# Attention scores from float32r parts: Q and K split into high and rest from batch 1 on

## The chip, the cores and the metric

The kernel runs on one core of a Trainium2 chip. Its engines are TensorE (PE in the profile, with its weight loads as PEld), VectorE (DVE), ScalarE (ACT), GpSimd (POOL) and SyncE (SP, which only issues DMAs here). Each engine works through its own instructions in order, and semaphores tie them together. The metric is the device time of one execution in microseconds (us); before the change it is 1247.83 us, the median of 3 runs (1247.72 to 1249.23).

## The reference

Sparse attention, then a gated feed-forward block. For 8 batches of 8 heads, 576 tokens and head size 64:

```python
scores = (1.0 / np.sqrt(D)) * np.matmul(q, k.transpose(0, 1, 3, 2))
kth = np.partition(scores, -32, axis=-1)[..., -32:-31]
scores = np.where(scores >= kth, scores, -1000000000.0)   # the 32 largest of each row stay
attn = np.exp(scores - np.max(scores, axis=-1, keepdims=True))
attn = attn / (np.sum(attn, axis=-1, keepdims=True) + 1e-09)
x = np.matmul(attn, v)                  # heads side by side: 4608 x 512
a, b = x @ w1, x @ w2                   # 4608 x 1024 each
out = (a * b @ w3) @ w_out              # 4608 x 512
```

The scores decide which 32 keys of a row are kept, so they are needed at nearly the precision of float32.

## The kernel before, in words

**Slots and turns.** A head pair (two heads, in the lower and upper 64 partitions) is handled in tiles of 128 tokens. A batch's 576 tokens are cut in two parts, of 320 and of 256. A part of 320 gives each head pair two tiles of 128 and half of one that it shares with the next head pair (`t == 4`, where two pairs bring 64 tokens each); a part of 256 gives two tiles. So a batch has 18 slots, two of them with `t == 4`, and there are 144 slots in all. The main loop (L541) runs one turn per slot, with a pipeline over the turns: in turn p the scores of slot p+1 are computed, the 32 largest of slot p are searched, slot p-1 is masked and exponentiated, and slot p-2 is transposed and multiplied with V.

**What a turn does.** In the order of the code: GpSimd makes the two `edge` values of slot p-1 from its largest scores. ScalarE's two `pab<-s` activations and GpSimd's two `pab<-s,pab` subtractions are the masks (`mask`, L303), one for each head. TensorE transposes slot p-2 (`tp`, `ro<-ident`), and ScalarE copies the result (`pts`, `pr`). ScalarE's two `pab<-pab,edge` activations are the exponentials. Then come the scores of slot p+1 (`st`, two PSUM tiles, for keys 0 to 383 and 384 to 575), their copies by ScalarE to `s`, the products with V (`ro`), and GpSimd's `sums` and its two `pab<-pab,sums` (normalise). VectorE's search (`w`, `top`) is laid between these steps.

**What fills TensorE.** The feed-forward block of a finished part is a queue of matmuls (`ab` and `eo`). `fill` (L497) is called three times in a turn and issues products up to a share that is counted in columns (`SHARE`, L41), not in time. So the number and order of TensorE's instructions in a turn are fixed when the program is built. What is left in the queue after the last slot runs at the end.

**The precision of the products.** The feed-forward block already works on parts: a float32 value is split into a high part rounded to float32r (a cast by ScalarE) and the rest (a subtraction), and a product is the sum of three float32r products, high by high, high by rest and rest by high. The scores are plain float32 products (L227 and L230): the Q tile is the stationary operand, 64 partitions by 128 tokens, and the K tile is streamed, 384 or 192 columns. Each of them shows up as two MATMUL instructions in the trace, a float32r product as one.

**Loads and buffers.** `load_qk` (L198) fetches a unit (a head pair of a part) into `qt` and `kt` (three buffers each). Its call is two turns ahead of the turn that computes the unit's first scores, and SyncE, which only waits for free buffers and for outputs to store, runs ahead of that. The `z` pool (L84, four buffers of 128 x 1024) holds the encoded weights in the first part of the run, up to the last weight load.

Nearly all instructions are recorded through one helper, so that they stand under line 54 in the profile; tiles tell them apart.

Of the kernel before, what the change touches and what calls it, by code (L numbers as in the profile page):

```python
# [9 lines left out]
F32 = mybir.dt.float32  # L10
F32R = mybir.dt.float32r
# [3 lines left out]
ALU = mybir.AluOpType  # L15
# [3 lines left out]
B, H, S, D = 8, 8, 576, 64  # L19
# [4 lines left out]
NA, NB = 320, 256  # L24
PARTS = ((0, NA, (0, 1, 4)), (NA, NB, (2, 3)))
PLACE = {0: 0, 1: 128, 4: 256, 2: 0, 3: 128}
HEADS = slice(0, 64), slice(64, 128)
# [35 lines left out]
def attn_moe(ctx: ExitStack, tc: tile.TileContext, q, k, v, w1, w2, w3, w_out, out, flag, general):  # L63
# [12 lines left out]
    pe, act, dve, pool, sp = nc.tensor, nc.scalar, nc.vector, nc.gpsimd, nc.sync  # L76
# [7 lines left out]
    z_p = ctx.enter_context(tc.tile_pool(name="z", bufs=4))  # L84
# [21 lines left out]
    if not general:  # L106
        pe, act, dve, pool, sp = (InOrder(tc, e) for e in (pe, act, dve, pool, sp))
# [87 lines left out]
    def at(x, b, *i):  # L195
        return x[(b, *i)] if isinstance(b, int) else x[(ds(b, 1), *i)].rearrange("o p n -> (o p) n")

    def load_qk(b, part, hp):  # L198

        lo, n, _ = PARTS[part]  # L200
        qt = kq_p.tile([128, NA], F32, tag="q", name="qt")
        sp.dma_start(qt[:, :n], at(q, b, hp)[:, lo : lo + n])
        kt = kq_p.tile([128, S + 64], F32, tag="k", name="kt")
        sp.dma_start(kt, at(k, b, hp))
        return qt, kt

    def load_v(b, hp):

        vt = kq_p.tile([128, 11 * D], F32, tag="v", name="vt")
        sp.dma_start(vt, at(v, b, hp))  # L210
        return vt

    def scores(pairs, t):

        out = []
        for lo, hi in KEYS:  # L220
            st = ps_a.tile([128, 2, 512], F32, tag="a", name="st")
            for a in range(2):
                cut = slice(lo + 64, hi + 64) if a == 0 else slice(lo, hi)
                if t == 4:
                    qt, kt = pairs[a]
                    for i, p in enumerate(HEADS):
                        pe.matmul(st[HEADS[i ^ a], a, : hi - lo], qt[p, PLACE[4] : NA], kt[p, cut], start=True, stop=True)  # L227
                else:
                    (qt, kt), p, o = pairs[0], HEADS[a], PLACE[t]
                    pe.matmul(st[:, a, : hi - lo], qt[p, o : o + 128], kt[p, cut], start=True, stop=True)  # L230
            out.append(st)
        return out

    def new_s():
        return att_p.tile([128, 2, S], F32, tag="s", name="s", bufs=2)
# [11 lines left out]
    def top32_steps(s, st, taken, slot):  # L247

        w = att_p.tile([128, 2, S], F32, tag="w", name="w", bufs=1)
        top = tops[slot % len(tops)]
        one, two, three = slice(0, NG), slice(NG, 2 * NG), slice(2 * NG, S)
        in_two, in_three = st[0][:, :, NG : 2 * NG], st[1][:, :, :NG]
        dve.tensor_tensor(w[:, :, three], s[:, :, one], in_two, op=ALU.max)
        dve.tensor_tensor(w[:, :, two], s[:, :, one], in_two, op=ALU.min)
        yield  # L260
        ins = dve.tensor_tensor(w[:, :, one], w[:, :, three], in_three, op=ALU.max)
        behind(ins, taken, "one engine at a time reads a bank of the scores")
        dve.tensor_tensor(w[:, :, three], w[:, :, three], in_three, op=ALU.min)
        yield
        for i in range(4):
            cut = slice(i * 8, (i + 1) * 8)
            for a in range(2):
                dve.max(top[:, a, cut], w[:, a, one] if i < 3 else w[:, a, :])
                if i == 3 and a == 0:
                    yield  # L270
            if i < 3:
                for a in range(2):
                    dve.match_replace(w[:, a, one], top[:, a, cut], w[:, a, one], NEG)
                yield

    def edges_of(slot):
        top = tops[slot % len(tops)]
        edge = small.tile([128, 2, 2], F32, tag="edge", name="edge")
        pool.tensor_tensor(edge, top[:, :, 0:32:31], coef, op=ALU.mult)
        return edge  # L280

    def compare(slot):
        top = tops[slot % len(tops)]
        pool.tensor_tensor(over[:, 2 * slot : 2 * slot + 2], top[:, :, 31], top[:, :, 23], op=ALU.subtract)
# [15 lines left out]
    def new_weights():  # L300
        return att_p.tile([128, 2, S], F32, tag="pab", name="pab"), small.tile([128, 2], F32, tag="sums", name="sums")
# [54 lines left out]
    def places(xs, t):  # L356
        o = PLACE[t]
        if t == 4:
            return [(x, slice(o, o + 64), slice(j * 64, j * 64 + 64)) for j, x in enumerate(xs)]
        return [(xs[0], slice(o, o + 128), slice(0, 128))]  # L360
# [5 lines left out]
    def take_low(to, ov):  # L366
        for x, cols, n in to:
            dve.tensor_tensor(x[:, 1, cols], ov[:, n], x[:, 0, cols].bitcast(F32), op=ALU.subtract)
# [78 lines left out]
    if general:  # L447
# [3 lines left out]
        with tc.For_i(0, B, 1) as b:  # L451
            seen = small.tile([1, 1], I32, tag="seen", name="seen", bufs=1)
            nc.sync.dma_start(seen, flag[ds(b + 1, 1), :])
            with tc.If(nc.values_load(seen, min_val=0, max_val=1) > 0):
                for part in range(2):
                    qk, vts, xs = {}, {}, {}
                    for of, hps, t in SLOTS:
# [5 lines left out]
                        s, st = new_s(), scores([qk[hp] for hp in hps], t)  # L463
# [12 lines left out]
                        to = places([xs[hp] for hp in hps], t)  # L476
# [7 lines left out]
    units = list(dict.fromkeys(u for us, _ in slots for u in us))  # L484
    first = {u: next(i for i, (us, _) in enumerate(slots) if u in us) for u in units}
    final = {(b, part): max(i for i, (us, _) in enumerate(slots) if us[0][:2] == (b, part)) for b in range(B) for part in range(2)}
    qk, vts, ss, sts, edges, pabs, xts, lows = {}, {}, {}, {}, {}, {}, {}, {}
    queue = []

    put_off = []  # L490
    spare = 0

    def evict():
        while put_off:
            put_off.pop(0)()

    def fill(n):  # L497
        nonlocal spare
        evict()
        spare = spare + n if queue else 0  # L500
        while queue and spare > 0:
            cost = next(queue[0], None)
            if cost is None:
                queue.pop(0)
            elif not cost:
                spare = 0
            else:
                spare -= cost
# [32 lines left out]
    for p in range(-1, n_slots + 3):  # L541
        i, j, m = p + 1, p - 1, p - 2
        if i < n_slots:
            for u in units:
                if first[u] - 2 == i:
                    qk[u] = load_qk(*u)
                if first[u] == i:
                    vts[u] = load_v(u[0], u[2])
        finder = top32_steps(ss[p], *sts.pop(p), p) if 0 <= p < n_slots else iter(())
        if 0 <= j < n_slots:  # L550
            edges[j] = edges_of(j)
        next(finder, None)
        if m - 1 in lows:
            take_low(*lows.pop(m - 1))
            b, part, _ = slots[m - 1][0][0]
            if final[b, part] == m - 1:
                queue.append(moe_steps(b, part, [xts.pop((b, part, hp)) for hp in range(NHP)], put_off.append))
        next(finder, None)
        if p >= 0:
            warm()  # L560
        if 0 <= j < n_slots:
            pabs[j] = new_weights()
            for a in range(2):
                mask(ss[j], edges[j], pabs[j][0], a)
            compare(j)
        fill(SHARE[0])
        next(finder, None)
        if 0 <= m < n_slots:
            tp, ro = turn(pabs[m][0])
            pts, pr = take_turned(tp, ro)  # L570
        warm(False)
        if 0 <= j < n_slots:
            exps(edges[j], *pabs[j], 0)
            exps(edges[j], *pabs[j], 1)
            enlarge(pabs[j][1])
        weigh(2)
        fill(SHARE[1])
        next(finder, None)
        warm(False)
        if i < n_slots:  # L580
            st = scores([qk[u] for u in slots[i][0]], slots[i][1])
            ss[i] = new_s()
            take_scores(ss[i], st, 0)
            sts[i] = st, take_scores(ss[i], st, 1)
        if 0 <= m < n_slots:
            us, t = slots[m]
            for u in us:
                if u not in xts:
                    xts[u] = new_x()
            ov = values([vts[u] for u in us], t, pts, pr, ro)  # L590
            lows[m] = places([xts[u] for u in us], t), ov
            take_high(*lows[m])
        next(finder, None)
        warm()
        next(finder, None)
        if 0 <= j < n_slots:
            invert(pabs[j][1])
            normalise(*pabs[j])
        weigh(8)
        fill(SHARE[2])  # L600
        for _ in finder:
            pass
        if 0 <= m < n_slots:
            del ss[m], pabs[m], edges[m]
        warm()
# [62 lines left out]
```

## Time and profile before

| | us |
|---|---|
| median of 3 runs | 1247.83 |
| the profiled execution | 1246.48 |
| its span, first to last instruction | 1244.6 |
| TensorE busy in the span | 1202.3 (97%) |
| VectorE busy | 1137.1 (91%) |
| ScalarE busy | 941.0 (76%) |
| GpSimd busy | 869.4 (70%) |

The profiled execution lies 1.35 us under the median, and its span 1.88 us under its own time. The first two hundred microseconds or so hold batch 0 and the loading of the weights; after that the turns repeat, batch by batch. Busy time of TensorE is a loose measure, since matmuls are pipelined and their ends are modelled, so durations of products overlap; the distance from the start of one to the start of the next tells their pace.

### The profile page before, as it was taken

To read this page: it belongs to the slowest core of one execution; us is meant where nothing else is said; L and a number is where in the kernel's file an instruction comes from. 1 tells how busy PE (TensorE), PEld (TensorE's weight loads), DVE (VectorE), ACT (ScalarE), POOL (GpSimd) and SP (SyncE) were. 2 spreads that over 40 slices of the span, in tenths; PEclk is the share of its full clock that TensorE was granted. 3 is DMA by queue.
4 is the path that set the end of the run, shared out by engine and by line. 5 is a ranking of instruction groups with operands and counts; after the bars stand their busy time and mean duration, and the time that the engine had idled before them with its cause. 6 is when DMAs were issued, how large, how long until landed. Compare 5 with 4: busy or idle time off the path is not lost.

```text
span 1244.6 us, 29906 instructions
## 1 busy us (share of the span) xinstructions
PE 1202.3 (97%) x10513; PEld 1042.5 (84%) x10513; DVE 1137.1 (91%) x3963; ACT 941.0 (76%) x2025; POOL 869.4 (70%) x1218
## 2 busy tenths in 40 slices
PE   4889799999999999999999999999999999999998
PEld 2444678898888888898889988888888988888998
DVE  7999999999999999999999999999999999999910
ACT  6888877787877777777777777777877777777731
POOL 6899887776767677676767667676767677676721
PEclk9999899999999999999999999999999999999999
DMA  6545411202121211213121121202112111202000
GB/s 230 190 145 178 140 56 39 72 28 93 40 67 53 71 56 35 71 33 94 41 66 54 48 80 33 73 28 89 49 46 75 40 61 39 92 28 71 13 23 21
DMA packets 42802, 85.91 MB, mean 69 GB/s; under 512 B 4754, under 2 KB 21138, under 8 KB 42642
## 3 DMA queue, kind: packets, MB, share of 16 engines
q1 hardware_dynamic: 42642, 83.91, 21.1%
q8 instruction: 85, 1.39, 0.5%
q14 instruction: 75, 0.61, 0.2%
HBM read 74.45 MB, written 9.44 MB: 67 GB/s over the span
## 4 chain that ended last, share of the span: by engine, by line
PE 91%; DVE 3%; POOL 2%; ACT 2%; issue 1%; DMA 1%; SPq 0%; ACTq 0%; DVEq 0%
PE ab L54 33%; PE eo L54 17%; PE ro L54 15%; PE st L54 13%; PE tp L54 10%; PE pf L54 3%; POOL pab L54 1%; DVE w L54 1%; DVE top L54 1%; DVE y L54 1%; DVE wl L54 1%; POOL y L54 1%; ACT pab L54 0%; POOL wo L54 0%; ACT s L54 0%
## 5 line engine op out<-in xcount | busy, mean ns | idle before, releaser
L54 POOL TENSOR_TENSOR pab<-s,pab 128x576 f32<-128x576 f32 x288 | 406.3, 1432 | 118.9 <-ACT pab L54 118.9
L54 DVE MAX8 top<-w 128x8 f32<-128x192 f32 (+1 forms) x1152 | 477.9, 447 | 0.0
L54 PE MATMUL ab<-xf,wh 128*128 128x256 f32 (+1 forms) x2048 | 439.0, 302 | 3.3 <-ACT asb L54 3.0
L54 PEld LDWEIGHTS ab<-xf,wh 128*128 128x128 f32 x2048 | 333.7, 189 | 14.5 <-issue 8.9
L54 PE MATMUL ab<-xf,wl 128*128 128x256 f32 (+1 forms) x1024 | 308.0, 301 | 0.0
L54 ACT ACTIVATE pab<-s,edge 128x576 f32<-128x576 f32 x288 | 208.0, 770 | 123.1 <-POOL edge L54 123.1
L54 DVE MATCH_REPLACE8 w<-top,w 128x192 f32<-128x192 f32 x864 | 289.3, 342 | 0.0
L54 POOL TENSOR_SCALAR pab<-pab,sums 128x576 f32<-128x576 f32 x288 | 211.6, 748 | 32.8 <-DVE sums L54 32.8
L54 PE MATMUL eo<-g,wf 128*128 128x256 f32 (+1 forms) x1536 | 231.6, 301 | 0.0
L54 ACT COPY pts<-tp 128x1024 f32<-128x1024 f32 x144 | 146.1, 1014 | 106.4 <-PE tp L54 106.1
L54 ACT ACTIVATE pab<-pab,edge 128x576 f32<-128x576 f32 x288 | 222.0, 779 | 4.0 <-POOL pab L54 3.8
L54 PEld LDWEIGHTS eo<-g,wf 128*128 128x128 f32 x1536 | 208.4, 188 | 8.1 <-issue 7.5
L54 PEld LDWEIGHTS ab<-xf,wl 128*128 128x128 f32 x1024 | 193.8, 189 | 4.1 <-issue 4.1
L54 PE MATMUL st<-kt,qt 64*128 64x192 f32 (+3 forms) x1280 | 181.7, 433 | 6.9 <-DMA kt<-in_k 4.3
L54 ACT COPY s<-st 128x768 f32<-128x768 f32 (+1 forms) x288 | 170.5, 650 | 4.0 <-PE st L54 4.0
L54 PE MATMUL tp<-ident,pab 128*128 128x128 f32 x1152 | 151.5, 275 | 18.2 <-DVE w L54 18.2
L54 DVE TENSOR_TENSOR w<-s,st 128x384 f32<-128x384 f32 x288 | 146.5, 550 | 21.4 <-ACT s L54 6.9
L54 PEld LDWEIGHTS st<-kt,qt 64*128 64x128 f32 (+1 forms) x1280 | 97.6, 178 | 77.7 <-issue 17.0
L54 DVE TENSOR_TENSOR w<-w,st 128x384 f32<-128x384 f32 x288 | 157.9, 548 | 4.9
L54 PE MATMUL ro<-pts,vt 128*64 128x128 f32 (+1 forms) x2560 | 160.4, 268 | 0.0
L54 PEld LDWEIGHTS tp<-ident,pab 128*128 128x128 f32 x1152 | 133.8, 142 | 24.7 <-POOL pab L54 15.4
L54 PEld LDWEIGHTS ro<-pts,vt 128*64 128x64 f32 x2560 | 126.8, 137 | 33.1 <-issue 31.6
(48 smaller groups left out, 1097.8 us busy)
## 6 DMA issues: line engine op xcount, KB each, us to landing
vt<-in_v SPq DMA_DIRECT2D x64, 352.0 KB, 3.2
kt<-in_k SPq DMA_DIRECT2D x64, 320.0 KB, 3.9
z<-in_w SPq DMA_DIRECT2D x32, 512.0 KB, 3.7
qt<-in_q SPq DMA_DIRECT2D x32, 160.0 KB, 3.2
out_t<-osb SPq DMA_DIRECT2D x32, 160.0 KB, 1.8
z<-in_wo SPq DMA_DIRECT2D x8, 512.0 KB, 5.6
qt<-in_q SPq DMA_DIRECT2D x32, 128.0 KB, 3.2
out_t<-osb SPq DMA_DIRECT2D x32, 128.0 KB, 1.7
```

Source lines behind the costliest of these rows:

```text
L54: ins = fn(*args, **kw)
```

## The change

Batch 0 stays as it is. From batch 1 on each unit gets two more tiles, `hi` and `lo`, in the `z` pool (128 x 1024, float32r; K stands in columns 0 to 639, Q behind it). One turn before the turn that computes the unit's first scores, ScalarE casts K to `hi` ahead of the masks (`split_k`) and Q after them (`split_q`), and GpSimd writes K's rest to `lo` ahead of its masks (`rest_k`). In the turn of the scores itself GpSimd writes Q's rest, again ahead of its masks (`rest_q`). The scores of those units become three products for each head and each of the two key ranges; slots with `t == 4` keep the float32 products.

```diff
-        return qt, kt
+        return [qt, kt, None, None]
+    def split_k(n, unit):
+        unit[2:] = (z_p.tile([128, 1024], F32R, tag="z", name=name) for name in ("hi", "lo"))
+        act.copy(unit[2][:, : S + 64], unit[1])
+    def split_q(n, unit):
+        act.copy(unit[2][:, S + 64 : S + 64 + n], unit[0][:, :n])
+    def rest_k(n, unit):
+        pool.tensor_tensor(unit[3][:, : S + 64], unit[1], unit[2][:, : S + 64].bitcast(F32), op=ALU.subtract)
+    def rest_q(n, unit):
+        cut = slice(S + 64, S + 64 + n)
+        pool.tensor_tensor(unit[3][:, cut], unit[0][:, :n], unit[2][:, cut].bitcast(F32), op=ALU.subtract)
...
-                    (qt, kt), p, o = pairs[0], HEADS[a], PLACE[t]
-                    pe.matmul(st[:, a, : hi - lo], qt[p, o : o + 128], kt[p, cut], start=True, stop=True)
+                    jobs.append((st[:, a, : hi - lo], pairs[0], HEADS[a], slice(PLACE[t], PLACE[t] + 128), cut))
+            for k in range(3):
+                for to, (qt, kt, high, low), p, tokens, keys in jobs:
+                    if high is not None and t != 4:
+                        q_at = slice(S + 64 + tokens.start, S + 64 + tokens.stop)
+                        q_part, k_part = (low if k == 1 else high)[p, q_at], (low if k == 2 else high)[p, keys]
+                        pe.matmul(to, q_part, k_part, start=(k == 0), stop=(k == 2))
+                    elif k == 0:
+                        pe.matmul(to, qt[p, tokens], kt[p, keys], start=True, stop=True)
...
+    parted = [u for u in units if u[0] > 0]
...
+        for u in parted:
+            if first[u] - 1 == i:
+                split_k(PARTS[u[1]][1], qk[u])
+        for u in parted:
+            if first[u] - 1 == i:
+                rest_k(PARTS[u[1]][1], qk[u])
+        for u in parted:
+            if first[u] - 0 == i:
+                rest_q(PARTS[u[1]][1], qk[u])
...
+        for u in parted:
+            if first[u] - 1 == i:
+                split_q(PARTS[u[1]][1], qk[u])
```

The first fence is TensorE's order at the scores of the first slot of batch 1, before (-) and after (+). `x2` counts the two heads; a float32 row of the score is two instructions in the trace. `hi,lo` is K's high part by Q's rest, `lo,hi` K's rest by Q's high part.

```order
 L54 MATMUL ab<-xf,wl_1527 128x320
 L54 MATMUL ab<-xf,wh_102 128x320
-L54 MATMUL st<-kt,qt 128x384 x2
-L54 MATMUL st<-kt,qt 128x192 x2
+L54 MATMUL st<-hi 128x384 x2
+L54 MATMUL st<-hi,lo 128x384 x2
+L54 MATMUL st<-lo,hi 128x384 x2
+L54 MATMUL st<-hi 128x192 x2
+L54 MATMUL st<-hi,lo 128x192 x2
+L54 MATMUL st<-lo,hi 128x192 x2
 L54 MATMUL ro<-pts,vt 64x128 x8
 L54 MATMUL ro<-pr,vt 64x128 x2
```

Four float32 products became twelve float32r products at the same place, between the feed-forward products ahead of them and the products with V behind them; nothing else moved on TensorE.

The next two fences are GpSimd's order over the two turns in which that unit is split, first of the kernel before.

```order
L54 TENSOR_TENSOR edge<-top_98,coef 128x4
L54 TENSOR_TENSOR pab<-s,pab 128x576 x2
L54 TENSOR_TENSOR over<-top_98 128x2
L54 TENSOR_SCALAR sums<-sums 128x2
L54 TENSOR_TENSOR g<-whole,g 128x320
L54 TENSOR_SCALAR pab<-pab,sums 128x576 x2
L54 TENSOR_TENSOR edge<-top_99,coef 128x4
L54 TENSOR_TENSOR pab<-s,pab 128x576 x2
```

And of the changed kernel:

```order
L54 TENSOR_TENSOR edge<-top_98,coef 128x4
L54 TENSOR_TENSOR lo<-kt,hi 128x640
L54 TENSOR_TENSOR pab<-s,pab 128x576 x2
L54 TENSOR_TENSOR over<-top_98 128x2
L54 TENSOR_SCALAR sums<-sums 128x2
L54 TENSOR_TENSOR g<-whole,g 128x320
L54 TENSOR_SCALAR pab<-pab,sums 128x576 x2
L54 TENSOR_TENSOR edge<-top_99,coef 128x4
L54 TENSOR_TENSOR lo<-qt,hi 128x320
L54 TENSOR_TENSOR pab<-s,pab 128x576 x2
```

K's rest stands between the edges and the masks of one turn, Q's rest between those of the next, and all that follows on GpSimd is queued behind them.

The last two fences are ScalarE's order in the first of these two turns, of the kernel before:

```order
L54 CAST xf<-ro 128x128
L54 COPY asb<-ab 128x320
L54 ACTIVATE pab<-s,edge 128x576 x2
L54 COPY pts<-tp 128x1024
L54 COPY pr<-ro 128x128
L54 ACTIVATE pab,sums<-pab,edge 128x576 x2
```

And of the changed kernel:

```order
L54 CAST xf<-ro 128x128
L54 COPY asb<-ab 128x320
L54 CAST hi<-kt 128x640
L54 ACTIVATE pab<-s,edge 128x576 x2
L54 CAST hi<-qt 128x320
L54 COPY pts<-tp 128x1024
L54 COPY pr<-ro 128x128
L54 ACTIVATE pab,sums<-pab,edge 128x576 x2
```

The cast of K stands ahead of the masks' activations, the cast of Q between them and the copy of the transposed tile. VectorE's and SyncE's orders are the same in both kernels.

## Rows read from the trace of the kernel before

**Rows 1.** The page: busy time, share of the span and instructions of each engine.

```profile
PE 1202.3 (97%) x10513; PEld 1042.5 (84%) x10513; DVE 1137.1 (91%) x3963; ACT 941.0 (76%) x2025; POOL 869.4 (70%) x1218
```

**Rows 2.** Windows: one batch; busy us of PE, PEld, DVE, ACT, POOL; granted clock; DMA.

```profile
480.40:622.00 141.60, 141.60 (x1299) 126.64 (x1298) 136.06 (x488) 110.06 (x241) 98.97 (x143) 1.00 0.18 57
```

**Rows 3.** Chain that ended last, in order of time: start us, us, engine, work, count.

```profile
606.35 1.17 PE st L54 x8
607.52 1.24 PE ro L54 x20
...
611.75 0.87 PE tp L54 x8
...
619.61 0.87 PE tp L54 x8
```

**Rows 4.** Timeline of PE, three places: start us, us, engine, operation, shape, count.

```profile
59.46 1.88 PE L54 MATMUL pf<-wo,y 128*128 128x512 f32 x4
61.18 1.04 PE L54 MATMUL tp<-ident,pab 128*128 128x128 f32 x8
...
610.12 0.31 PE L54 MATMUL ab<-xf,wl 128*128 128x320 f32 x1
610.27 0.46 PE L54 MATMUL ab<-xf,wh 128*128 128x320 f32 x2
610.56 0.31 PE L54 MATMUL ab<-xf,wl 128*128 128x320 f32 x1
...
1227.62 11.67 PE L54 MATMUL eo<-g,wf 128*128 128x256 f32 x96
```

**Rows 5.** Groups by shape: busy us, mean ns of one | idle before, its releasers.

```profile
L54 POOL TENSOR_TENSOR g<-whole,g 128x320 fp32r<-128x320 f32 x64 | 56.0, 875 | 2.0
...
L54 POOL TENSOR_TENSOR g<-whole,g 128x256 fp32r<-128x256 f32 x64 | 47.0, 735 | 34.0 <-ACT g L54 32.3
...
L54 ACT CAST g<-whole 128x320 fp32r<-128x320 f32 x64 | 30.0, 469 | 4.8 <-DVE whole L54 4.8
...
L54 ACT CAST wh<-y 128x512 fp32r<-128x512 f32 x16 | 10.0, 626 | 8.6 <-POOL y L54 8.6
...
L54 POOL TENSOR_TENSOR wl<-y,wh 128x512 fp32r<-128x512 f32 x4 | 5.2, 1288 | 0.0
```

**Rows 6.** Waits, 197 to 1172 us: who waited for whom, us, times, longest.

```profile
ACT pab L54 <- POOL edge L54: 111.4, 124, 1.7
POOL pab L54 <- ACT pab L54: 110.3, 124, 0.9
ACT pts L54 <- PE tp L54: 99.0, 123, 1.5
```

**Rows 7.** Timeline of one turn, all engines; in brackets the idle time before.

```profile
610.26 0.21 POOL L54 TENSOR_TENSOR edge<-top,coef 128x4 f32<-128x4 f32 x1
...
610.50 1.45 ACT L54 ACTIVATE pab<-s,edge 128x576 f32<-128x576 f32 x2 [1.02 <-POOL edge L54]
...
611.36 2.81 POOL L54 TENSOR_TENSOR pab<-s,pab 128x576 f32<-128x576 f32 x2 [0.89 <-ACT pab L54]
...
614.55 0.77 ACT L54 ACTIVATE pab<-pab,edge 128x576 f32<-128x576 f32 x1
...
615.62 1.20 ACT L54 COPY s<-st 128x768 f32<-128x768 f32 x2
...
616.02 1.47 POOL L54 TENSOR_SCALAR pab<-pab,sums 128x576 f32<-128x576 f32 x2 [0.29 <-DVE sums L54]
...
616.68 1.02 DVE L54 TENSOR_TENSOR w<-s,st 128x384 f32<-128x384 f32 x2
...
617.45 0.19 POOL L54 TENSOR_TENSOR edge<-top,coef 128x4 f32<-128x4 f32 x1
...
618.53 2.81 POOL L54 TENSOR_TENSOR pab<-s,pab 128x576 f32<-128x576 f32 x2 [0.89 <-ACT pab L54]
```

**Rows 8.** Timeline of SyncE's queue: when a load of K is issued.

```profile
586.09 0.43 SPq L54 DMA_DIRECT2D kt<-in_k  x1
```

More of the change, by code (lines that the diff above doesn't have):

```diff
@@ L221, in scores @@
             st = ps_a.tile([128, 2, 512], F32, tag="a", name="st")
+            jobs = []
             for a in range(2):
@@ L224, in scores @@
                 if t == 4:
-                    qt, kt = pairs[a]
                     for i, p in enumerate(HEADS):
-                        pe.matmul(st[HEADS[i ^ a], a, : hi - lo], qt[p, PLACE[4] : NA], kt[p, cut], start=True, stop=True)
+                        jobs.append((st[HEADS[i ^ a], a, : hi - lo], pairs[a], p, slice(PLACE[4], NA), cut))
                 else:
-                    (qt, kt), p, o = pairs[0], HEADS[a], PLACE[t]
-                    pe.matmul(st[:, a, : hi - lo], qt[p, o : o + 128], kt[p, cut], start=True, stop=True)
+                    jobs.append((st[:, a, : hi - lo], pairs[0], HEADS[a], slice(PLACE[t], PLACE[t] + 128), cut))
[7 more added lines that the diff above has]
+                        pe.matmul(to, qt[p, tokens], kt[p, keys], start=True, stop=True)
             out.append(st)
```

## The prediction

> **What bounds the kernel now.** I read the page's busy times first: TensorE stands at 97%, VectorE at 91%, GpSimd at 70% [rows 1]. These are means over a loading phase and a steady one, so the second view is the windows, of one whole batch in the steady part: TensorE is busy for all 141.60 us, VectorE for 136.06, ScalarE for 110.06, GpSimd for 98.97, at a granted clock of 1.00, the level of 2.4 GHz [rows 2]. Busy TensorE may hide gaps, so the third view is the chain of waits over that stretch: it goes from TensorE work to TensorE work and leaves it nowhere, scores 1.17 us, products with V 1.24, transposes 0.87, feed-forward products between, and it repeats every 7.86 us (transposes at 611.75 and 619.61) [rows 3]. So from batch 1 on the time is TensorE's own work, laid end to end. The list of waits shows who has room: GpSimd's edge is waited for by ScalarE 0.90 us a turn (111.4 over 124), ScalarE's mask activation by GpSimd 0.89, the transposes by ScalarE's copy 0.80 [rows 6]. VectorE has least: 5.54 us in a batch of 18 turns, 0.31 a turn [rows 2].
>
> **TensorE's part of the change.** Of 18 slots in a batch 16 take the new products; over batches 1 to 7 that is 112 turns. What goes are four float32 products a turn, eight instructions. Their pace comes from a plain run of float32 products of 512 columns: four instructions between 59.46 and 61.18, 0.43 us each, 0.84 ns a column [rows 4]. A head's 576 columns take two such instructions each, 2 x 576 x 0.84 ns = 0.968 us. Two heads one after the other would be 1.94, more than the 1.17 us that the whole stretch lasts [rows 3], so the heads, in different halves of the array, run side by side; 0.20 us are left for the start and the end, which I keep.
>
> What comes are three pairs of 384 columns and three of 192, one instruction per product. Float32r paces in the trace: three products of 320 columns between 610.12 and 610.56, 0.147 us each; 96 of 256 columns in 11.67 us with a last one that is modelled long, 0.120 each [rows 4]. That is 0.42 ns a column and 13 ns per product, so 384 columns take 0.1735. For 192 columns no row exists. The same line gives 0.093, as the lower end. But each product loads 128 columns of weights first, and the nearest row with so short a stream behind such a load is the transposes, 0.87 us for 8, 0.109 each [rows 3]: I take that. The upper end is the pace at 256 columns, 0.120, since fewer columns need not be slower. Sum: 3 x 0.1735 + 3 x 0.109 = 0.848 us instead of 0.968, 0.120 saved a turn (0.088 to 0.168 between the ends), and times 112 that is 13.5 us (9.8 to 18.8). The scores thus shrink by an eighth, not by the quarter that three passes for four suggest, because the narrow products are held by their weights.
>
> The Trainium skill (FP8 and Floating Point Precision, section TensorE Precision Notes) counts true float32 as four passes through the array, and the reduced form as one. By that count three products are three quarters of the streaming time, the result of the third rival below; no row here shows a narrow float32r product, so the trace has not decided it.
>
> **ScalarE's part.** Each of 56 units adds two casts. From 0.469 us at 320 columns and 0.626 at 512 [rows 5], 0.82 ns a column, K's 640 columns take 0.73 and Q's 320 take 0.47. K's cast stands where ScalarE waits for the edges: 1.02 us ahead of 610.50, 0.90 in the mean [rows 6, 7]; Q's where it waits for the transposes, 0.80 in the mean. Both are covered in a usual turn, so I cost them at nothing; without cover they would delay the masks by 0.73 and the copies by 0.47. What K's cast reads was fetched long before: the load for the slot whose K is split near 610 was issued at 586.09 [rows 8]. No DMA is added or moved, and SyncE's order stays.
>
> **GpSimd's part.** From 0.875 us at 320 columns and 1.288 at 512 [rows 5], 2.15 ns a column, K's rest takes 1.56 us and Q's 0.875 (0.735 for 256 columns): 8 x 2.37 = 18.9 us more a batch, 117.9 of 139.7. There is room in sum; the question is the place. Take the turn of [rows 7]. GpSimd's edges end at 610.47, its masks start at 611.36, after 0.89 of waiting for ScalarE. K's rest from 610.47 ends at 612.03, so the masks come 0.67 late and end at 614.84 instead of 614.17. Queued behind them on GpSimd are the sums and the normalising; waiting elsewhere is ScalarE's second exponential, at 614.55 until now, which comes 0.29 late, and behind it the copies of the scores (615.62, ending 616.82), from which VectorE starts its next search at 616.68. At the worst all 0.29 arrive there. Per batch that is 8 x 0.29 = 2.3 us, against VectorE's 5.54 less the 16 x 0.120 = 1.9 by which the batch gets shorter: 3.6 remain. Normalising, which ends at 617.49, moves to 617.78, and TensorE's transposes of that slot come at 619.61 [rows 3]: 1.8 us of cover. A turn later Q's rest ends 0.875 after the edges (617.64), at 618.52, where the masks start at 618.53 anyway, so the lag doesn't grow and is worked off. I cost GpSimd's part at nothing; the ends are nothing and the case of the second rival.
>
> **The sum.** Against the profiled execution: 1246.48 - 13.5 = 1233.0. The median of the runs lies 1.35 above that execution, so 1234 in the runs' terms. The likeliest case by itself is 1229 to 1238.
>
> **The rivals.**
> - VectorE becomes the bound. For: its 0.31 us a turn are the smallest room of all, and K turns come every other turn. Against: the sum above leaves 3.6 us a batch. If more than 0.45 us (3.6 / 8) of a K turn arrives at VectorE, the gain starts to go; at about 0.57, half is left, 1241; at the full 0.67 the batch is 136.06 + 8 x 0.67 = 141.4, no change, 1246 to 1248.
> - Slower by GpSimd's place: K's rest ahead of the masks isn't covered at all, because K's cast (0.73 against 0.90 of room in the mean [rows 6]) comes late in turns where ScalarE has less, and edge, cast, rest and masks become one string. Then 1.56 us arrive per K turn: 136.06 + 12.5 = 148.5 a batch, 6.9 over before, times 7 batches 48: 1296. It turns slower from 0.69 us per K turn on. For: the order of both engines is strict. Against: 0.89 of the 1.56 lies in a wait that every turn has [rows 6]. Its middle is near 1265.
> - The quarter: every product costs its columns' share alone, 3 x 576 x 0.42 ns, and the streaming shrinks from 0.968 to 0.726, 0.242 a turn, 27.1 us: 1221. Against: it needs 192 columns below the pace of the transposes.
> - Slower by the product itself: a float32r product on 64 partitions, or under 256 columns, could take as long as a float32 one. No row excludes it: every float32r product of the trace uses 128 partitions and 256 or 320 columns [rows 4]. With 3 x 0.322 for the narrow ones (192 columns at 2 x 0.84 ns) the scores take 0.52 + 0.97 = 1.49, 0.52 more a turn, 58 us: 1306. If the two heads no longer ran side by side, it would be worse.
> - The change doing less than it says: the slots with `t == 4` keep float32 by the code, and are left out above.
>
> **How the numbers follow.** Forecast 0.58; VectorE bound with part of the gain left 0.11, with none left 0.06; GpSimd's place, slower, 0.12; the quarter 0.04; slow narrow products 0.09. What a measurement here can tell from no change is about 0.2%, 2.5 us. So faster 0.58 + 0.11 + 0.04 = 0.73, the same 0.06, slower 0.21. The range reaches from 1227, which leaves out the quarter (0.04), to 1255, which leaves out the slow products (0.09) and about half of GpSimd's case (0.06).
>
> **What would show it.** In the profile of the changed kernel the scores' piece of the chain should last about 1.05 us instead of 1.17, three narrow pairs should follow each other at 0.11, the batch should last about 139.7 us with TensorE still busy throughout, and VectorE's idle time should shrink to some 3 us or less. `lo<-kt` should take 1.56 us, with the masks of that turn late by 0.7, and those of the next on time. The prediction is wrong if the chain leaves TensorE in the steady part for GpSimd's masks or VectorE's search, or if the narrow pairs come at 0.2 us or more.

## The result, and the profile after

The changed kernel takes 1231.96 us (median of 4 runs, 1231.67 to 1232.23) against 1247.78 (4 runs, 1247.04 to 1249.23): a ratio of 0.9876, 95% interval 0.9863 to 0.9889, so 13.9 to 17.1 us less, 15.8 in the medians. The forecast was 1234, its range 1227 to 1255. The profiled execution took 1231.92 us, its span 1230.1.

First the page's line of busy times, to be read against [rows 1], and then a window of one whole batch of the changed kernel, the same 18 turns as [rows 2] (busy us of PE, PEld, DVE, ACT, POOL, with instructions; granted clock; DMA).

```profile
PE 1187.3 (97%) x10961; PEld 1069.0 (87%) x10961; DVE 1134.5 (92%) x3963; ACT 997.3 (81%) x2137; POOL 996.4 (81%) x1330
```

```profile
476.70:615.90 139.20, 139.20 (x1363) 130.44 (x1362) 135.44 (x487) 117.94 (x257) 116.99 (x159) 1.00 0.19 58
```

A batch lasts 139.2 us instead of 141.6, at the same clock. TensorE is still busy in all of it; GpSimd has 18.0 us more, ScalarE 7.9. From the scores of one batch's first slot to those of the next it is 139.25 us instead of 141.55: 2.30 us, or 0.144 for each of the 16 turns with the new products. Over the run: the scores of slot 18, the first of batch 1, start 1.0 us later than before (190.4 against 189.5), those of slot 126 start 12.9 earlier, those of slot 143, the last, 15.0. Of that 0.5 goes behind the last scores, and 14.5 is what the two spans differ by (1244.6 to 1230.1).

The chain of waits in the changed kernel, against [rows 3]:

```profile
600.55 1.03 PE st L54 x9
601.58 1.24 PE ro L54 x20
...
605.81 0.87 PE tp L54 x8
...
608.27 1.03 PE st L54 x10
```

Only the scores are shorter, 1.03 us instead of 1.17; the turn is 7.72 long (600.55 to 608.27). From batch 1 on the chain leaves TensorE in one place, where that of the kernel before stays on it, from 1132.9 to 1172.5 us:

```profile
1131.94 0.89 PE tp L54 x8
...
1132.91 1.02 ACT pts L54
...
1138.68 1.52 POOL lo L54
...
1145.57 1.02 DVE w L54 x2
...
1172.55 1.31 PE ro L54 x20
```

These are the last turns with scores and the first without. Once no scores are left, a turn of TensorE is shorter (6.7 us, 1180.43 to 1187.11 in the kernel before), and the chain runs through ScalarE, a rest of K on GpSimd and VectorE's search, which end later than TensorE needs. With it goes the 0.5 us just named: from the start of the last scores to the end it is 72.7 us, before 72.1.

TensorE's timeline near 600 us shows the three wide and the three narrow pairs (start, us, shape, count; the distance between starts is the pace):

```profile
600.49 0.44 PE L54 MATMUL st<-hi 64*128 64x384 f32 x2
600.76 0.33 PE L54 MATMUL st<-hi,lo 64*128 64x384 f32 x2
600.94 0.34 PE L54 MATMUL st<-lo,hi 64*128 64x384 f32 x2
601.11 0.26 PE L54 MATMUL st<-hi 64*128 64x192 f32 x2
601.20 0.27 PE L54 MATMUL st<-hi,lo 64*128 64x192 f32 x2
601.31 0.27 PE L54 MATMUL st<-lo,hi 64*128 64x192 f32 x2
601.51 0.66 PE L54 MATMUL ro<-pts,vt 128*64 128x128 f32 x8
```

The wide pairs follow each other at 0.18 and 0.17, the narrow ones at 0.09 and 0.11, and both heads go in one step: they do run side by side. The new work on the other engines, by shape (busy us, mean ns of one, idle before), 197 to 1160 us, GpSimd's first and then ScalarE's:

```profile
L54 POOL TENSOR_TENSOR lo<-kt,hi 128x640 fp32r<-128x640 f32 x54 | 85.1, 1577 | 0.0
L54 POOL TENSOR_TENSOR lo<-qt,hi 128x320 fp32r<-128x320 f32 x27 | 23.7, 879 | 0.0
```

```profile
L54 ACT CAST hi<-kt 128x640 fp32r<-128x640 f32 x54 | 41.3, 766 | 0.0
L54 ACT CAST hi<-qt 128x320 fp32r<-128x320 f32 x26 | 11.5, 442 | 0.0
```

And the waits of the same stretch (who waited for whom, us, times, longest), to be read against [rows 6]:

```profile
ACT pab L54 <- POOL edge L54: 90.9, 118, 1.5
ACT pts L54 <- PE tp L54: 33.5, 62, 1.0
POOL pab L54 <- ACT pab L54: 18.8, 43, 0.9
ACT pab L54 <- POOL pab L54: 15.2, 46, 0.5
DVE sums L54 <- POOL sums L54: 6.4, 19, 0.5
```

GpSimd's 110 us of waiting for the masks' activations have shrunk to 19: that gap now holds the rests. ScalarE's wait for the transposes fell from 99 to 34, since it arrives later. New is the fourth line: in 46 turns an exponential stands waiting for its mask. Up to the last scores none of this reaches TensorE, but some of it comes close. One place, in GpSimd's and then in TensorE's weight loads' timeline of the changed kernel:

```profile
603.97 1.48 POOL L54 TENSOR_SCALAR pab<-pab,sums 128x576 f32<-128x576 f32 x2
605.40 0.21 POOL L54 TENSOR_TENSOR edge<-top,coef 128x4 f32<-128x4 f32 x1
```

```profile
605.50 0.94 PEld L54 LDWEIGHTS tp<-ident,pab 128*128 128x128 f32 x8
```

The same two steps of the same turn in the kernel before:

```profile
608.83 1.48 POOL L54 TENSOR_SCALAR pab<-pab,sums 128x576 f32<-128x576 f32 x2
```

```profile
611.45 0.94 PEld L54 LDWEIGHTS tp<-ident,pab 128*128 128x128 f32 x8
```

The transposes load what normalising leaves. Before, normalising ended at 610.31 and the load began 1.14 us later; now it ends at 605.45, and the load begins at 605.50. So 0.05 us are left in this turn; the same place of the other batches has 0.01 to 0.05. The edges behind it come 4.85 us after the start of the scores (605.40 less 600.55), where it was 3.91 (610.26 less 606.35 [rows 3, 7]): the lateness of the turns ahead was not worked off here. The experiments ask how much of the gain that endangers.

### The profile page after: what moved, and what is told of

The parts are those of the page before. It is cut to its first block, busy times and chain, and to the rows that moved or that the text cites. A ratio compares the mean times of both kernels' runs of the same rounds, so it can differ in the third digit from the quotient of the medians.

```text
span 1230.1 us, 31107 instructions
## 1 busy us (share of the span) xinstructions
PE 1187.3 (97%) x10961; PEld 1069.0 (87%) x10961; DVE 1134.5 (92%) x3963; ACT 997.3 (81%) x2137; POOL 996.4 (81%) x1330
## 4 chain that ended last, share of the span: by engine, by line
PE 88%; DVE 5%; POOL 3%; ACT 2%; issue 1%; DMA 1%; SPq 0%; ACTq 0%; DVEq 0%
PE ab L54 32%; PE eo L54 17%; PE ro L54 14%; PE st L54 11%; PE tp L54 9%; PE pf L54 4%; DVE w L54 2%; DVE top L54 1%; POOL pab L54 1%; POOL y L54 1%; DVE y L54 1%; ACT pab L54 1%; DVE wl L54 1%; POOL wo L54 1%; ACT pts L54 0%
## 5 line engine op out<-in xcount | busy, mean ns | idle before, releaser
L54 POOL TENSOR_TENSOR g<-whole,g 128x256 fp32r<-128x256 f32 (+1 forms) x128 | 103.4, 808 | 35.8 <-ACT g L54 32.1
L54 POOL TENSOR_SCALAR sums<-sums 128x2 f32<-128x2 f32 x144 | 31.0, 216 | 105.5 <-ACT pab L54 102.8
```

Source lines behind the costliest of these rows:

```text
L54: ins = fn(*args, **kw)
```

## The experiments

Every experiment is the changed kernel with one edit. The theory: the gain is TensorE's score products alone, all added work is covered, and the cover is nearly used up.

**1. The parts made, not used.**

```diff
-                    if high is not None and t != 4:
+                    if high is not None and t > 4:
```

> All casts and rests of the changed kernel are made, but the scores stay the float32 products of the kernel before. Theory (TensorE sets the time, the new work of ScalarE and GpSimd is covered): 1247.8 us, as before, within 2.5 us; a batch lasts 141.6 us and the scores' piece 1.17 us. Rival (the covered work does cost, and the changed kernel gained more on TensorE than 15.8 us and gave some back): 1251 to 1262 us, and a batch over 142.2 us.

Measured: 1247.71 us (10 runs), a ratio to the kernel before of 0.9999 (0.9989 to 1.0008). Its batch:

```profile
480.50:622.10 141.60, 141.60 (x1301) 126.70 (x1300) 135.90 (x487) 118.01 (x257) 117.00 (x159) 1.00 0.18 57
```

ScalarE and GpSimd do all the new work, and the batch is the one of before to 0.1 us. So the added work costs nothing in a batch, and all of the gain comes from the products.

**2. The products alone.** Later units use the parts of the first.

```diff
-        for u in parted:
+        for u in parted[:1]:
...
+        for u in parted[1:]:
+            if first[u] - 1 == i:
+                qk[u][2:] = qk[parted[0]][2:]
```

> Only the first unit of batch 1 is split; all later units take its high and rest tiles in their three products, so their scores are those of other heads. This is the change without its work on ScalarE and GpSimd. Theory (TensorE alone sets the time): 1232 us, as the changed kernel, within 2.5 us; a batch 139.2 us, GpSimd back at about 99 us busy in it. Rival (casts and rests hold something up): 1220 to 1228 us.

Measured: 1230.18 us (1229.39 to 1232.18), ratio 0.9861 (0.9843 to 0.9878).

```profile
474.90:614.10 139.20, 139.20 (x1363) 130.48 (x1362) 135.30 (x487) 110.00 (x241) 98.93 (x143) 1.00 0.19 58
```

Without the casts and rests a batch takes the same 139.2 us as with them. The difference to the changed kernel, 1.8 us in the medians and 2.0 in the two spans, lies outside the batches: 1.7 of it ahead of slot 18 (its scores start at 188.7 against 190.4), where the two kernels do the same work, and 0.3 behind the last scores. Experiments 1 and 2 together are the two halves of the theory, and both hold.

**3. One product instead of three.**

```diff
-                        pe.matmul(to, q_part, k_part, start=(k == 0), stop=(k == 2))
+                        if k == 0:
+                            pe.matmul(to, q_part, k_part, start=True, stop=True)
```

> Of the three products only high by high is computed; casts and rests stay. It leaves out two thirds of the new scores' work to find what lies behind TensorE. TensorE's work in a batch falls by 16 x 0.54 = 8.6 us to 130.6. Theory (VectorE, 136.1 us busy in a batch before, is the next bound): a batch 136 to 137 us and 1211 to 1217 us, VectorE without idle time. Rival 1 (TensorE stays the bound): 1172 us. Rival 2 (GpSimd's string of edge, rest, masks, sums and normalising is the next bound, ahead of VectorE): a batch of 138 us or more, 1222 us or more, with TensorE or VectorE waiting for GpSimd.

Measured: 1226.34 us, ratio 0.9828 (0.9812 to 0.9845).

```profile
474.50:613.00 138.50, 135.10 (x1237) 121.23 (x1236) 135.13 (x488) 117.52 (x257) 116.73 (x159) 1.00 0.19 58
```

Two thirds of the score products are gone, and a batch is 0.7 us shorter. TensorE now idles 3.4 us of a batch; its weight loads for the transposes wait for GpSimd's normalising (20.2 us, 33 times, 210 to 1160 us). The theory and rival 1 failed, and rival 2's numbers came: right behind TensorE stands the next bound, at about 138.5 us a batch. Whether it is GpSimd's string, as rival 2 has it, the next run asks.

**4. One product, no casts or rests** (experiments 2 and 3 together).

> Only high by high is computed, and later units take the first unit's tiles, so neither casts nor rests load ScalarE and GpSimd: two thirds of the new products are left out and scores are those of other heads. TensorE's work is 130.6 us a batch. Theory (with casts and rests, GpSimd's string stops the kernel with one product at 138.3 us a batch; without them VectorE does, at its 135.4 to 136.5): 1207 to 1215 us, VectorE without idle time. Rival (something else holds it at 138 us): 1222 us or more.

Measured: 1217.93 us (1217.75 to 1219.03), ratio 0.9761 (0.9745 to 0.9778).

```profile
471.80:609.30 137.50, 134.25 (x1236) 120.77 (x1235) 134.66 (x487) 109.85 (x241) 98.84 (x143) 1.00 0.19 59
```

The time lies between what the theory and the rival said, nearer to the theory. With GpSimd at 98.8 the batch is still 137.5, so the new work is worth only 1.0 us of the bound behind TensorE; most of that bound was there before the change. VectorE is busy for 134.7 and TensorE for 134.3. The chain of waits over this batch names the one that sets the 137.5; its shares, by engine and tile:

```profile
by line: DVE w L54 49.9%; DVE top L54 36.6%; issue 5.2%; DVE whole L54 4.5%; DVE xf L54 2.7%; DVE sums L54 1.1%; DVEq L54 0.3%
```

It never leaves VectorE: the steps of the search, of the feed-forward block and the reciprocals stand end to end, with gaps (`issue`) in which VectorE waited for nothing that the profile shows. So the theory had the right engine, and its price was too low: VectorE's string takes 137.5 us (137.25 in the mean of six batches) for 134.7 of busy time. The changed kernel's 139.25 leave it some 2.0 us a batch, not the 3.8 in which it is idle there.

**5. Narrow products cut to 64 columns.** The second and third narrow product only.

```diff
+                        if k and lo:
+                            to, k_part = to[:, :64], k_part[:, :64]
```

> In the range of 192 keys the second and third products stream only 64 columns (they leave out 128 keys of that range). Theory (behind the first narrow pair the pace is set by loading 128 columns of weights): the distance from the second narrow pair to the third stays 0.10 us, and only the last pair ends earlier, so the scores' piece shrinks by about 0.05 us to 0.98 and the time falls by 5 to 6 us to 1226 or 1227. Rival (columns set the pace of narrow pairs too): both pairs shrink by 128 x 0.42 ns, the distance falls to 0.05 us, the piece to 0.92 us, and the time to 1220, or to where GpSimd's string stops it.

Measured: 1227.91 us (1226.03 to 1229.36), ratio 0.9839 (0.9822 to 0.9855); a batch takes 138.5. TensorE's timeline:

```profile
599.20 0.21 PE L54 MATMUL st<-hi,lo 64*128 64x64 f32 x2
599.25 0.27 PE L54 MATMUL st<-lo,hi 64*128 64x64 f32 x2
599.45 1.09 PE L54 MATMUL ro<-pts,vt 128*64 128x128 f32 x16
```

From the second narrow pair to `ro` it is 0.25 us instead of 0.31: 0.06 less, where 256 columns fewer at the 0.42 ns of [rows 4] would give 0.107. The distance from the second pair to the third fell from 0.11 to 0.05, by about what 128 columns take, where the theory had it stay, so by the starts columns set the pace there. What did not shrink is the way from the last pair to `ro`, 0.20 us behind 192 columns and behind 64. What fills it is open: the load of 128 columns of weights with a record that begins early (the third pair's is the longer, 0.27 against 0.21), or the change from the scores to the products with V. The piece lasts 0.97 us, near the theory's 0.98 and not the rival's 0.92, but the theory's mechanism is not shown by that. The time fell by 4.0 us and not by 5 to 6, since one turn of a batch got longer (7.87 us for 7.71). The Trainium skill (TensorE: Matmul & The Clock Gate, section LDWEIGHTS) gives a load P/1.2 ns for P columns, 107 ns for 128; the changed kernel's narrow pairs follow each other at 0.09 and 0.11 and the pairs of 64 columns at 0.05, so the distances do not bear it out as a lower limit, and no run here measures a load by itself.

**6. K's rest twice.**

```diff
                 rest_k(PARTS[u[1]][1], qk[u])
+                rest_k(PARTS[u[1]][1], qk[u])
```

> K's rest is computed twice, one behind the other, so that GpSimd's masks come 1.56 us later still in every second turn. GpSimd's busy time in a batch rises to about 130 us of 139.2. Theory (the cover of the rest ahead of the masks is nearly used up in the changed kernel: GpSimd idles 0.4 to 0.9 us in turns with a K rest and 0.4 to 1.9 in those with a Q rest): 1236 to 1250 us. Rival 1 (there is ample cover): 1232 us. Rival 2 (all of it is exposed, 56 x 1.56 us): 1300 us or more.

Measured: 1316.46 us, ratio 1.0548 (1.0530 to 1.0565). The theory's 1236 to 1250 failed, and rival 2's 1300 or more came. A batch, the chain of waits in one K turn, and the waits (210 to 1250 us):

```profile
502.70:653.80 151.10, 142.69 (x1365) 130.49 (x1364) 135.62 (x487) 118.16 (x258) 129.25 (x167) 1.00 0.17 54
```

```profile
500.27 0.87 PE tp L54 x8
...
501.27 1.57 POOL lo L54
502.84 2.76 POOL pab L54 x2
...
506.67 0.22 POOL sums L54
507.00 0.49 DVE whole L54
```

```profile
DVE sums L54 <- POOL sums L54: 88.3, 54, 2.1
...
PE tp L54 <- DVE w L54: 23.8, 40, 1.5
...
PEld tp L54 <- POOL pab L54: 17.2, 16, 1.7
```

A second 1.58 us in 8 turns of a batch made it 11.9 longer, 1.49 each. The chain, which stays on TensorE in the changed kernel's turns, now goes through the rest, the masks, `sums` and then VectorE, though no engine is full: TensorE 142.7 of 151.1, VectorE 135.6, GpSimd 129.3. What binds is the order of the steps, not the load of an engine.

**7. The same with the link from GpSimd's sums to VectorE cut.** VectorE inverts sums that are a slot old; the kernel of experiment 6 otherwise.

```diff
+                rest_k(PARTS[u[1]][1], qk[u])
...
-            invert(pabs[j][1])
-            normalise(*pabs[j])
+            ready = pabs[m if m >= 0 else j][1]
+            invert(ready)
+            normalise(pabs[j][0], ready)
```

> K's rest is computed twice as before, 1316.5 us, but VectorE inverts the sums of the slot before, which are long there, and the normalising takes those: the weights of a tile are divided by another tile's sums. So VectorE's reciprocal no longer waits for GpSimd's sums of the same turn. Theory (late masks reach VectorE by that reciprocal, for which it waited 88.3 us in the kernel with the rest twice): most of the 84 us go, 1235 to 1265 us, and the wait of VectorE for the sums is gone. Rival (late masks reach it by ScalarE, whose exponentials wait for the masks and hold up the copies of the scores and of the feed-forward products behind them): 1290 us or more, with the lost time in waits for ScalarE's copies.

Measured: 1302.35 us (1299.95 to 1303.15), ratio 1.0430 (1.0411 to 1.0448). VectorE's wait for the sums, 88.3 us in experiment 6, is gone, and with it only 14 of the 84 us: the rival came, not the theory. The waits (210 to 1160 us) name the other ways by which late masks travel:

```profile
ACT pab L54 <- POOL pab L54: 105.8, 126, 1.7
...
DVE w L54 <- ACT s L54: 47.5, 32, 1.7
PEld ab L54 <- ACT asb L54: 29.7, 32, 1.8
```

ScalarE stands at an exponential until its mask is there. Queued behind that exponential are the copies of the scores, from which VectorE searches, and of the feed-forward products (`asb`), whose PSUM TensorE needs. A late mask so reaches two engines that don't read it.

**8 and 9. A little more on GpSimd.** An extra subtraction of 128 columns, then of 320, behind K's rest; 0.46 and 0.88 us in the traces.

```diff
+                hi, lo = (x[:, :128] for x in qk[u][2:])
+                pool.tensor_tensor(lo, qk[u][1][:, :128], hi.bitcast(F32), op=ALU.subtract)
```

> The changed kernel with one more GpSimd subtraction, of 128 columns of K's rest, right behind the rest itself, in each of the 56 turns with a K rest; by the subtractions of 1.58 us at 640 columns and .88 at 320 (intercept .18, 2.2 ns a column) some .46 us. It leaves out nothing (the columns are only written again). Theory: masks and what ScalarE has queued behind them have next to no room left in these turns (the doubled rest was exposed by 1.50 of its 1.56 us), so .40 of .46 shows, 56 x .40 = 22 us: 1250 to 1257. Rival: the loss of the doubled rest set in only late, small lateness is absorbed by ScalarE's and TensorE's room: 1231 to 1238. A loss in between says that the room is between none and .46 us, by its share of 26 us.

> The same with 320 columns, some .88 us in each of the 56 turns; leaves out nothing. Theory: all but .06 us of it shows, 56 x .82 = 46 us: 1272 to 1282. Rival: room of half a microsecond first, 56 x .4 = 22: 1250 to 1262. The two runs together give the loss as a line: where it crosses zero is the room that the changed kernel has left.

Measured: 1254.70 us (1253.69 to 1255.41), ratio 1.0044 (1.0030 to 1.0058), and 1277.45 (1277.01 to 1277.90), ratio 1.0228 (1.0211 to 1.0245). One batch of each:

```profile
483.70:626.10 142.40, 140.77 (x1365) 130.26 (x1364) 135.55 (x487) 118.18 (x257) 120.61 (x167) 1.00 0.19 57
```

```profile
490.70:636.40 145.70, 142.02 (x1363) 130.45 (x1362) 135.60 (x487) 118.22 (x257) 123.92 (x167) 1.00 0.18 56
```

With experiment 6 that is a line. Per K turn, an extra 0.46, 0.88 and 1.58 us cost 0.40, 0.81 and 1.49 (3.2, 6.5 and 11.9 a batch, over 8): all but 0.06 to 0.09 us shows. The theory's numbers held. It is a mean: of the eight K turns some still absorb the 0.46, and others lose more than it. Waits of the 128-column run (210 to 1160 us):

```profile
DVE sums L54 <- POOL sums L54: 28.3, 53, 1.0
...
PE tp L54 <- DVE w L54: 4.9, 18, 0.4
...
PEld tp L54 <- POOL pab L54: 3.9, 7, 0.6
```

The last one is the 0.05 us of the section above: it ran out at that place in six batches, and once elsewhere. TensorE's transposes wait more often for VectorE's search, 18 times, the line above it.

**10. K's rest behind the masks instead of ahead.**

```diff
-            if first[u] - 1 == i:
-                rest_k(PARTS[u[1]][1], qk[u])
...
+        for u in parted:
+            if first[u] - 1 == i:
+                rest_k(PARTS[u[1]][1], qk[u])
```

> K's rest stands behind the masks instead of ahead of them, so the masks come on time and the sums and the normalising wait for it. Theory (TensorE sets the time as long as GpSimd's string of edge, rest, masks, sums and normalising fits into the turns, and it just fits): 1232 us, a batch 139.2 us. Rival 1 (the place costs the changed kernel something): 1226 to 1229. Rival 2 (the normalising comes too late for the transposes or the next edge): 1236 to 1260.

Measured: 1244.52 us (10 runs), ratio 0.9975 (0.9965 to 0.9984): 12.6 of the 15.8 us are lost, and rival 2 came. A batch is 141.0, and two turns, 8.7 and 8.0 long instead of 7.7, hold most of it. Ahead of the masks part of the rest fills GpSimd's wait for ScalarE (19 us in the changed kernel); behind them that wait is empty again (66 us), and all of the rest's 1.58 us stands ahead of the sums.

**11. K's rest by VectorE.**

```diff
-        pool.tensor_tensor(unit[3][:, : S + 64], unit[1], unit[2][:, : S + 64].bitcast(F32), op=ALU.subtract)
+        dve.tensor_tensor(unit[3][:, : S + 64], unit[1], unit[2][:, : S + 64].bitcast(F32), op=ALU.subtract)
```

> K's rest is made by VectorE instead of GpSimd. By the 1.11 us that VectorE took for a rest of 512 columns, one of 640 takes 1.39 us, 11.1 us a batch. VectorE is busy 135.4 of the changed kernel's 139.2 us. Theory (VectorE then is the bound): a batch of 146.5 us, 1283 us. Rival (VectorE's busy time is partly waiting for others, and takes this in): 1232 to 1250 us.

Measured: 1263.16 us (1262.56 to 1264.33), ratio 1.0120 (1.0103 to 1.0137). A batch, and the new group on VectorE:

```profile
486.50:629.90 143.40, 142.13 (x1363) 130.20 (x1362) 140.91 (x495) 117.20 (x257) 107.08 (x151) 1.00 0.18 57
```

```profile
L54 DVE TENSOR_TENSOR lo<-kt,hi 128x640 fp32r<-128x640 f32 x53 | 45.5, 858 | 0.0
```

VectorE does become the bound, busy for 140.9 of 143.4 us, with nine tenths of the batch's chain on it, so the direction was right. The price was not: 0.86 us each, not the estimated 1.39, and the time fell between the two that were expected. VectorE is faster at this step than GpSimd, and still the wrong place for it.

No run here beats the changed kernel with the same output. Float32r products in the slots with `t == 4` were not tried.

## Why the prediction was right

**The bound and the mechanism held.** TensorE's work is laid end to end from batch 1 to the last scores, before and after; the gain is the shorter score piece times the turns, and all the rest is free there (experiments 1 and 2). The prediction's own sign of being wrong, a chain that leaves TensorE for GpSimd or VectorE, came only in the last turns, for 0.5 us.

**The saving of a turn was mis-sized**, 0.120 us for a measured 0.144 (13.8 us over the 96 turns between the scores of slots 18 and 126 that have the new products), so 13.5 for 16.1 over 112 turns. The score piece came out at 1.03 instead of 1.05, and its term was the narrow pairs: 0.109 was taken, 0.09 and 0.11 are measured. The wide pairs were right (0.1735; measured 0.17 to 0.18). "Held by their weights" is not shown: in experiment 5, by the starts, columns count from 192 down to 64. That the two spans differ by 14.5, nearer to the 13.5, is in part luck: the scores of slot 18 start 1.0 us later than before in the changed kernel's profile, and 0.8 earlier in that of experiment 2, which does the same work up to there.

**The quarter did not come.** Three products take about 0.14 us a turn less than the float32 ones did, not 0.242. The Trainium skill (FP8 and Floating Point Precision, section TensorE Precision Notes) counts four passes for float32. One pass for a float32r product is what the paces of [rows 4] say (0.42 ns a column against twice 0.84), and three of four would save a quarter of the streaming; the trace shows some 0.82 of 0.97 us left, a saving of 15%.

**The added work was priced well.** K's rest 1.577 us (1.56 said), Q's 0.879 (0.875), K's cast 0.766 (0.73), Q's 0.442 (0.47); GpSimd 117.0 a batch (117.9).

**The cover was read from the wrong turn.** The result does not show it, since nothing leaked, but two sentences failed. First, the masks were said to be 0.67 us late in K's turn and on time in the next, the lag "worked off". Counted from the start of the scores ahead of them, the masks of the turns with a rest of K came 0.57 to 1.56 us later than before, 0.84 in the mean, and those of the turns with a rest of Q 0 to 0.98 later, 0.43 in the mean. The lag is worked off wholly in one turn of a batch; over the turns around a batch's end it piles up. Second, "1.8 us of cover" ahead of the transposes came from the turn of [rows 7]; the turn just ahead of it had 1.14 before the change and has 0.05 now. For VectorE I had 0.45 us a K turn, less the 0.29 of the late exponential: 0.16 to spare. The line of experiments 6, 8 and 9 gives 0.06 to 0.09. The rival "Slower by GpSimd's place" had 0.12 and was nearer than it looked: its mechanism is real and starts right behind the changed kernel. It was also said to decide from VectorE's idle time; it works through ScalarE's queue, `sums` and the transposes as well, at a VectorE that has 15 us idle in a batch of experiment 6.

**VectorE's idle time** in a batch is 3.8 us (139.20 less 135.44), not "some 3 us or less"; before it was 5.54. The prediction took all of it for room. Experiment 4 shows that VectorE's own string needs 2.8 us a batch more than its busy time, so some 2.0 were left, where the sum had 3.6.

## What to carry to other kernels

Where one engine's work lies end to end, price the change on that engine by paces at the nearest shape and count turns; what other engines get cost nothing here as long as the latest of the steps that they release still arrived, so look for the smallest distance between a release and its use over all turns, not over one. An engine that is 84% busy, as GpSimd here, may have no room left: what it delivers late holds its reader at a wait, and with it everything queued behind that wait, also for engines that never read the late value. Idle time is not room either: with the whole chain on it, VectorE still took 137.5 us for 134.7 of busy time. Doubling the suspected step, and then adding a little to it, measures the room in two or three runs.

## What the runs showed of the hardware

- Float32r products on 64 partitions, two heads in the two halves of the array, run side by side: a pair of 384 columns in 0.17 us, of 192 in about 0.10.
- Two pairs of 64 columns began 0.05 us apart, and the next work came 0.20 after the second, as it did behind a pair of 192 columns. Paces are better read over several products than from one distance.
- VectorE's subtraction of two tiles of 128 x 640 took 0.82 us in the median (0.86 in the mean, up to 1.0) where GpSimd's took 1.58.
